# Alternating the score products, moving the weight decoding, and a shorter first pass in an mLSTM + two-layer MLP kernel

## The chip, the cores and the metric

One core of one Trainium2 chip. The metric is the device time of one launch in microseconds: the kernel before takes 467.19 us (median of three runs, 466.68 to 467.29).

## The reference

The inputs are q, k, v and o_gate of shape (2, 8, 768, 40) and i_gate, f_gate of shape (2, 8, 768). An mLSTM runs over the 768 steps of each of the 16 heads:

```
m_new = max(f + m, i);  f_stab = exp(f + m - m_new);  i_stab = exp(i - m_new)
C = f_stab * C + i_stab * outer(v, k)
n = f_stab * n + i_stab * k
y = sigmoid(o) * (C q) / max(|n q|, 1)
```

Its output, 1536 tokens of width 320, goes through two dense layers, each with weights 320 x 2048 in and 2048 x 320 out:

```
h = x @ w_in;  g = h - tanh(h);            x = g @ w_out      # layer 1
h = x @ w_in;  g = h * tanh(softplus(h));  x = g @ w_out      # layer 2
```

## The kernel before

**Attention.** The recurrence is done in chunks of 128 steps: 6 chunks of 2 batch entries make 12 token tiles, each with 8 heads. `attention(j)` (L279) does one of them. It makes the decay matrix in two halves (`nb`, L303 to L319, exponential on ScalarE, L322; mask on GpSimd, L324), the scores of the 8 heads into two PSUM tiles `sc` of 4 heads each (L339), multiplies them by the decay on VectorE (L343), adds the product with the carried state (`it`, L350) to the product with v (`pv`, L361), normalises and gates (L355 to L376; `gated[j]`, L374, is the last of these), and updates the state (`st`, L382; L389, L390). A q or k of heads 0 to 3 lies on partitions 0 to 63, one of heads 4 to 7 on partitions 64 to 127. So a score product uses one half of TensorE's rows, and the two `sc` tiles belong to the two halves. The inputs are float32, and each such product is two MATMUL instructions in the trace: 16 per token tile for the scores. From the MLP's start on, all PSUM tiles of the attention come from one pool of 3 buffers (`ps_at`).

**MLP.** Token tiles are grouped by two into 6 blocks for layer 1, and by four into 3 for layer 2. A weight part is 128 of the 2048 hidden units, 16 parts per layer. The work unit, called a tile here, is of the same size in both layers: in layer 1 a block of 256 tokens by 2 parts, in layer 2 512 tokens by 1 part, 48 of them per layer. For each, `mm1` (L506) makes the hidden values with 16 (layer 1) or 8 (layer 2) MATMULs of L516, `tile1` or `tile2` applies the activation on ScalarE and VectorE and splits the result in a high and a low part, and `mm2` (L561) multiplies by the out weights with 12 MATMULs (L577 to L579), two tiles later.

**Two passes.** Layer 1 goes over the blocks twice. `CUT` (L84) says how many parts a block takes in the first pass, and `segs` (L496) lists the stretches: first pass of blocks 0 to 5, then second pass of blocks 0 to 5 with the other parts. With 8 and 10 parts the first pass has 4 + 5 * 5 = 29 tiles and the second 19. In the first pass over block k the attention of block k+1 is emitted in between, 14 steps per stretch (`ahead`, L752, L794 and L823), since that block's transposed input `xT` (L264 to L267) must be there when the next stretch begins. The attention of block 0 comes before the first tile.

**Decoding.** A weight part arrives as float64 bits (704 KB) and is turned into a high and a low float32 part by `conv_w` (L180): four or five VectorE instructions (L190, L191, L194, L199, L200) with two ScalarE ones between (L192, L197). `conv_to` (L776) emits decodings: up to `CUT[0]` in the first stretch, then evenly over the first pass, `CY` tiles ahead; `mark` is VectorE's first instruction of the latest activation, and the decoding stands behind it in VectorE's queue. In the second pass it emits the first four parts of layer 2. After each decoding the next load is issued on SyncE's queue, into one of 3 buffers (`rawp`).

**Order.** The program is traced in the order of the code, and a planner with its own estimate of times then sets the order of each engine's queue: an instruction that comes later may go first if it is ready earlier. `issue_after` (in `after`, L135) ties an instruction behind another one on its engine; `in_turn` (L142) makes a chain of such ties. On the chip each engine runs its queue in that order.

Of the kernel before, what the change touches and what calls it, by code (L numbers as in the profile page):

```python
# [25 lines left out]
def kernel(  # L26
# [11 lines left out]
    nc = tc.nc  # L38
    B, P, _, HG, S = qk.shape
# [5 lines left out]
    NF, _, WC = w1.shape  # L45
    D1 = D + 1
    HP = P // 2
# [33 lines left out]
    NB = len(blocks1)  # L81


    CUT = [8] + [10] * (NB - 1)  # L84
    M1 = max(BLOCKS) * L
    M2 = max(len(x) for x in flat) * L
    MX = max(NP * M1, M2)
# [39 lines left out]
    last, chain, fill, mark, second = [], [], [], [], []  # L127
# [3 lines left out]
    scored, gated = {}, {}  # L131
# [3 lines left out]
    def after(x):  # L135
        e = ExitStack()
        for i in x:
            e.enter_context(tc.issue_after(i.ins))
        return e

    @contextmanager
    def in_turn(bound=True):  # L142
        done = []

        def turn(issue):
            with after(done[-1:] if bound else []):
                done.append(issue())

        yield turn

    def copy_r(eng, o, x):
        if eng == 0:
            nc.scalar.activation(out=o, in_=x, func=AF.Copy)  # L153
        elif eng == 1:
            nc.vector.tensor_copy(o, x)
        else:
            nc.gpsimd.tensor_scalar(o, in0=x, scalar1=1.0, scalar2=0.0, op0=ALU.mult, op1=ALU.add)
# [6 lines left out]
    def load_w(n=1):  # L164
        for _ in range(n):
            if pending_loads:
                layer, f = pending_loads.pop(0)
                early = layer == 0 and f < ER
                t = (xp if early else rawp).tile(
                    [P, 2 * WC], U32, tag="x" if early else "raw", name="raw", bufs=NB - 1 if early else None  # L170
                )
                with after(spq):
                    x = nc.sync.dma_start(out=t, in_=(w1, w2)[layer][f].bitcast(U32))
                if layer == 0 and f < ER + 3:
                    spq[:] = [x]
                raw[layer, f] = t
# [3 lines left out]
    def conv_w(layer, f, first=(), behind=()):  # L180
        r = raw.pop((layer, f)).rearrange("p (n t) -> p n t", t=2)
        lo32, z = r[:, :, 0], r[:, :, 1]
        zf = z.bitcast(F32)
        w = wp.tile([P, WT], F32R, tag="w", name="w")
        wf = w.bitcast(F32)

        with after(first):
            nc.vector.tensor_scalar(lo32, in0=lo32, scalar1=29, scalar2=None, op0=ALU.logical_shift_right)  # L190
        nc.vector.scalar_tensor_tensor(lo32, in0=z, scalar=0x80000000, in1=lo32, op0=ALU.bitwise_and, op1=ALU.bitwise_or)  # L191
        scaled[layer, f] = nc.scalar.activation(out=zf, in_=zf, func=AF.Copy, scale=2.0 ** -111)  # L192
        with after(behind):
            third[layer, f] = nc.vector.scalar_tensor_tensor(  # L194
                z, in0=z, scalar=3, in1=lo32, op0=ALU.logical_shift_left, op1=ALU.bitwise_or
            )
        cvd[:] = [nc.scalar.activation(out=w[:, 0:WC], in_=zf, func=AF.Copy)]  # L197
        eng = nc.gpsimd if layer == 0 and f < PRE else nc.vector
        eng.tensor_tensor(w[:, WC:WT], in0=zf[:, 0:REM0], in1=wf[:, 0:REM0], op=ALU.subtract)  # L199
        eng.tensor_tensor(w[64:P, REM0:REM1], in0=zf[64:P, REM0:REM1], in1=wf[64:P, REM0:REM1], op=ALU.subtract)  # L200
        wtile[layer, f] = w
# [27 lines left out]
    def load_o(c0, c1):  # L229
        x = xo[:, :, 0:DM].rearrange("p (c b) d -> p c b d", b=B)  # L230
        if c1 - c0 == 1:
            nc.sync.dma_start(out=x[:, c0, :, :], in_=og[:, c0 * L:c1 * L, :].rearrange("b s d -> s b d"))
            return
        for b in range(B):
            nc.sync.dma_start(
                out=x[:, c0:c1, b, :], in_=og[b, c0 * L:c1 * L, :].rearrange("(c s) d -> s c d", s=L)
            )
# [7 lines left out]
    def at_ps(shape, name):  # L245
        p, tag = at_pools[0]
        if len(at_pools) > 1:
            at_pools.append(at_pools.pop(0))
        return p.tile(shape, F32, tag=tag, name=name)
# [29 lines left out]
    def attention(j):  # L279
# [3 lines left out]
        hp = lambda t, h, d=D: t[HP * (h // HG):HP * (h // HG) + d, h % HG, :]  # L283
# [14 lines left out]
        for hf in range(2):  # L298
            nb = at_ps([P, HG, L], "nb")
            flat = nb.rearrange("p g s -> p (g s)")  # L300
            if c < EC:
                bh = b * H + HG * hf
                nc.tensor.matmul(  # L303
                    flat, lhsT=na[c], rhs=sel[:, bh:bh + HG].rearrange("p (g o) -> p g o", o=1).to_broadcast([P, HG, L]),
                    start=True, stop=False,
                )
                for hh in range(HG):
                    nc.tensor.matmul(
                        nb[:, hh, :], lhsT=sel[:, bh + hh:bh + hh + 1].to_broadcast([P, P]), rhs=n0[c], start=False,
                        stop=False,  # L310
                    )

                x = nc.tensor.matmul(
                    nb, lhsT=identr, rhs=cm.rearrange("p (o s) -> p o s", o=1).to_broadcast([P, HG, L]), start=False,
                    stop=True,
                )
# [13 lines left out]
        if c + 1 < NCH:  # L330
            wv = ap_.tile([P, H, D1], F32, tag="wv", name="wv", bufs=2)
# [1 line left out]
            copy_r(2, dl, Dm[:, :, L - 1:L])  # L333
            dls[:] = [nc.gpsimd.tensor_tensor(wv, in0=v, in1=dl.to_broadcast([P, H, D1]), op=ALU.mult)]
        scs = [at_ps([P, HG, L], "sc") for _ in range(2)]
        for hh in range(HG):
            for r, sc in enumerate(scs):
                h = HG * r + hh
                x = nc.tensor.matmul(sc[:, hh, :], lhsT=hp(kT, h, HP), rhs=hp(q, h, HP), start=True, stop=True)  # L339
        yield  # L340
        for r, sc in enumerate(scs):
            d4 = Dm[:, HG * r:HG * r + HG, :]
# [4 lines left out]
        if c > 0:  # L347
            it = at_ps([P, HG, 2, D1], "it")
            for g in range(HG):
                nc.tensor.matmul(  # L350
                    it[:, g].rearrange("p h d -> p (h d)"), lhsT=q[:, g, :],
                    rhs=C[:, g].rearrange("p h d -> p (h d)"), start=True, stop=True,
# [7 lines left out]
        for h in range(H):  # L360
            x = nc.tensor.matmul(pv[:, h, :], lhsT=Dm[:, h, :], rhs=v[:, h, :], start=True, stop=True)  # L361
# [3 lines left out]
        else:  # L365
# [6 lines left out]
        x = xo[:, j, 0:DM].rearrange("p (h d) -> p h d", h=H)  # L372
        nc.vector.tensor_tensor(x, in0=hv[:, :, 0:D], in1=x, op=ALU.mult)
        gated[j] = nc.vector.scalar_tensor_tensor(  # L374
            x, in0=x, scalar=1 / WS, in1=den.to_broadcast([P, H, D]), op0=ALU.mult, op1=ALU.mult
# [2 lines left out]
        yield  # L378
        if c + 1 < NCH:
            st = at_ps([P, HG, D1], "st")  # L380
            for h in [HG * r + g for g in range(HG) for r in range(2)]:
                nc.tensor.matmul(hp(st, h), lhsT=k[:, h, :], rhs=wv[:, h, :], start=True, stop=True)  # L382
            for r in range(2):
                sl = slice(HP * r, HP * r + D)
                if c == 0:
                    copy_r(0, C[sl, :, r, :], st[sl])
                else:
                    dc = dec[sl, b, :, c:c + 1].to_broadcast([D, HG, D1])
                    nc.gpsimd.tensor_tensor(C[sl, :, r, :], in0=C[sl, :, r, :], in1=dc, op=ALU.mult)  # L389
                    nc.vector.tensor_tensor(C[sl, :, r, :], in0=C[sl, :, r, :], in1=st[sl], op=ALU.add)  # L390
# [104 lines left out]

    segs = [(bi, 0, CUT[bi]) for bi in range(NB)] + [(bi, CUT[bi], NF) for bi in range(NB)]  # L496
    tiles = [(0, bi, f) for bi, f0, f1 in segs for f in range(f0, f1, NP)]
# [4 lines left out]
    def span(i):  # L502
        l, bi, f = tiles[i]
        return l, bi, range(f, f + (1 if l else NP)), len(blk[l, bi]) * L
# [27 lines left out]
    def tile1(i):  # L532
# [4 lines left out]

        with after(tbl + ([scaled[0, fs[-1] + 1]] if i < CUT[0] // NP - 1 else [])):
            texp.append(nc.scalar.activation(out=u, in_=h, func=AF.Tanh, scale=G_B))  # L539
# [21 lines left out]
    def mm2(i):  # L561
        l, bi, fs, nt = span(i)
        ends_ = (0,) if l else (0, CUT[bi], NF)
        if fs[0] in ends_:
# [15 lines left out]
        if fs[-1] + 1 in ends_ or fs[-1] == NF - 1:  # L580
            more = l == 0 and fs[-1] + 1 > CUT[bi]
            for t, a in enumerate(accs.pop((l, bi))):
# [27 lines left out]
    def program():  # L610
# [56 lines left out]
        new_xT(0, 0)  # L667

        ga, gb = (attention(j) for j in blk[0, 0])

        def go(g, n=1):
# [22 lines left out]
        start = chain[:]  # L694
        conv1 = [0]

        def lead1(n, x=()):
            while conv1[0] < min(n, NF):
                f = conv1[0]
                with after(x):  # L700
                    conv_w(
                        0, f, [third[0, f - 1]] if f and f < PRE else (), [gated[f]] if f < PRE else ()
                    )
                if conv1[0] >= PRE:
                    load_w()
                if conv1[0] == PRE + 1:
                    with after(spq):
                        load_o(*oc.pop(0))
                conv1[0] += 1
# [56 lines left out]
        seg_at, k = {}, 0  # L766
        for n, (_, f0, f1) in enumerate(segs):
            seg_at[k] = n
            k += len(range(f0, f1, NP))
        n_0 = sum(CUT) // NP  # L770
        n_s = CUT[0] // NP


        CY, R2, E2 = 6, 4, 4

        def conv_to(i, bi, f):  # L776
            if i < n_s:
                lead1(min(CUT[0], f + PRE + NP), start)
            elif i < n_0:
                lead1(CUT[0] + -(-(NF - CUT[0]) * min(i - n_s + CY, n_0 - n_s) // (n_0 - n_s)), mark)  # L780
            elif conv1[0] == NF:
                lead2(min((i - n_0 + 2) // R2, E2))

# [4 lines left out]
        for i in range(len(tiles)):  # L788
# [3 lines left out]
            if l == 0 and i in seg_at:  # L792
                k = seg_at[i]
# [105 lines left out]
```

## Time and profile before

| | us |
|---|---|
| median of three runs | 467.19 |
| the profiled execution | 467.56 |
| its span, first to last instruction | 465.5 |
| PE busy | 449.7 (97%) |
| DVE busy | 321.2 (69%) |
| ACT busy | 285.7 (61%) |
| POOL busy | 115.0 (25%) |

PE is TensorE, DVE VectorE, ACT ScalarE, POOL GpSimd, SP SyncE. The share of busy time is a mean over stages that differ, so it is read by stretches. 2.1 us of the profiled execution lie outside the span.

### The profile page before, as it was taken

The numbers are of one execution on the slowest core, as the hardware profiler recorded it, in microseconds if no ns is written. First come the engines' busy times: TensorE is split into PE (matmuls) and PEld (weight loads), VectorE is DVE, ScalarE is ACT, GpSimd is POOL, SyncE is SP. The second block draws the span as 40 slices with busy tenths as digits, with TensorE's granted clock in tenths as the row PEclk, the third lists the DMA queues.
The fourth block names the chain that finished last, engine by engine and source line by source line (L and its number), as shares of the span: only waits on it lengthen the run. The fifth ranks groups of instructions, "written<-read, shape, count | busy, mean of one in ns | idle before, by whom it ended". The sixth has DMA issues, their size and how long they took to land.

```text
span 465.5 us, 8005 instructions
## 1 busy us (share of the span) xinstructions
PE 449.7 (97%) x3103; PEld 407.8 (88%) x3103; DVE 321.2 (69%) x546; ACT 285.7 (61%) x518; POOL 115.0 (25%) x121
## 2 busy tenths in 40 slices
PE   9968979999999999999999999999999999999997
PEld 5645869999989999999999989988889988998896
DVE  7997999989888887666889977989943221221112
ACT  6878556596665865888889787666643322332232
POOL 3313535475354431342433332000000000000000
PEclk9999999999999999999999999999999999999999
DMA  7964453513506111000120110435301000010001
GB/s 249 353 246 155 144 164 128 179 37 108 165 4 182 29 63 63 1 1 1 63 64 0 63 63 1 131 127 182 121 1 56 2 0 1 0 58 0 1 0 56
DMA packets 22744, 38.03 MB, mean 82 GB/s; under 512 B 1364, under 2 KB 17044, under 8 KB 22708
## 3 DMA queue, kind: packets, MB, share of 16 engines
q1 hardware_dynamic: 22708, 37.54, 24.5%
q8 instruction: 24, 0.39, 0.3%
q14 instruction: 12, 0.10, 0.1%
HBM read 35.41 MB, written 1.97 MB: 80 GB/s over the span
## 4 chain that ended last, share of the span: by engine, by line
PE 64%; DVE 18%; issue 7%; ACT 4%; POOL 3%; DMA 2%; POOLq 0%; SPq 0%; ACTq 0%; DVEq 0%
PE h L516 28%; PE acc L577 9%; PE acc L578 9%; PE acc L579 9%; DVE raw L194 3%; PE sc L339 3%; POOL gl L529 3%; DMA raw<-in_w_dram 2%; PE pv L361 2%; DVE raw L191 2%; DVE w L199 2%; DVE raw L190 2%; DVE w L200 2%; DVE gl L558 1%; PE xt L264 1%
## 5 line engine op out<-in xcount | busy, mean ns | idle before, releaser
L516 PE MATMUL h<-xT,w 128*128 128x256 f32 (+1 forms) x1152 | 210.9, 323 | 7.5 <-ACT w L197 4.2
L516 PEld LDWEIGHTS h<-xT,w 128*128 128x128 f32 x1152 | 169.0, 189 | 25.5 <-ACT w L197 6.2
L577 PE MATMUL acc<-w,gh 128*128 128x320 f32 x384 | 118.6, 312 | 0.8 <-DVE xo L594 0.8
L578 PE MATMUL acc<-w,gh 128*128 128x320 f32 x384 | 118.2, 310 | 0.0
L579 PE MATMUL acc<-w,gl 128*128 128x320 f32 x384 | 109.9, 310 | 0.0
L529 POOL TENSOR_TENSOR gl<-g,gh 128x512 fp32r<-128x512 f32 x48 | 66.0, 1377 | 120.8 <-ACT gh L153 115.1
L558 DVE TENSOR_TENSOR gl<-g,gh 128x512 fp32r<-128x512 f32 x48 | 33.1, 691 | 86.8 <-ACT g L557 86.7
L577 PEld LDWEIGHTS acc<-w,gh 128*128 128x128 f32 x384 | 72.0, 188 | 3.5 <-ACT w L197 1.0
L556 ACT ACTIVATE gh<-h 128x512 fp32r<-128x512 f32 x48 | 28.8, 599 | 75.4 <-PE h L516 74.9
L578 PEld LDWEIGHTS acc<-w,gh 128*128 128x128 f32 x384 | 72.2, 188 | 2.3
L579 PEld LDWEIGHTS acc<-w,gl 128*128 128x128 f32 x384 | 69.7, 188 | 1.5 <-issue 0.4
L545 DVE COPY_PREDICATED g<-u,t 128x512 f32<-128x512 uint32 x48 | 40.5, 846 | 10.0 <-ACT u L544 9.9
L542 DVE TENSOR_TENSOR g<-u,h 128x512 f32<-128x512 f32 x48 | 32.7, 681 | 16.9 <-ACT u L541 13.4
L153 ACT ACTIVATE gh<-g 128x512 fp32r<-128x512 f32 x48 | 30.5, 635 | 19.7 <-DVE g L545 15.4
L544 ACT ACTIVATE u<-u,bias 128x512 f32<-128x512 f32 x48 | 34.9, 727 | 11.4 <-DVE g L542 11.4
L197 ACT ACTIVATE w<-raw 128x704 fp32r<-128x704 f32 x32 | 27.5, 861 | 16.2 <-DVE raw L194 16.0
L539 ACT ACTIVATE u<-h 128x512 f32<-128x512 f32 x48 | 28.5, 593 | 11.7 <-PE h L516 11.6
L192 ACT ACTIVATE raw<-raw 128x704 f32<-128x704 f32 x32 | 27.6, 864 | 11.1 <-DVE raw L191 10.0
L543 DVE TENSOR_TENSOR t<-h,t 128x512 f32<-128x512 f32 x48 | 32.8, 683 | 0.0
L194 DVE SCALAR_TENSOR_TENSOR raw<-raw 128x704 uint32<-128x704 uint32 x32 | 30.9, 964 | 2.6 <-ACT raw L192 2.4
L541 ACT ACTIVATE u<-u 128x512 f32<-128x512 f32 x48 | 30.6, 638 | 0.0
L199 DVE TENSOR_TENSOR w<-raw,w 128x576 fp32r<-128x576 f32 x30 | 27.5, 915 | 2.9 <-ACT w L197 2.4
(103 smaller groups left out, 496.8 us busy)
## 6 DMA issues: line engine op xcount, KB each, us to landing
raw<-in_w_dram SPq DMA_DIRECT2D x32, 704.0 KB
qk_t<-in_qk_dram SPq DMA_DIRECT2D x12, 512.0 KB
kv_t<-in_kv_dram SPq DMA_DIRECT2D x12, 324.0 KB
out_dram<-xo SPq DMA_DIRECT2D x12, 160.0 KB
xo<-in_og_dram SPq DMA_DIRECT2D x2, 640.0 KB
xo<-in_og_dram SPq DMA_DIRECT2D x2, 320.0 KB
sd<-nr SPq DMA_DIRECT2D x20, 4.0 KB
md<-nr SPq DMA_DIRECT2D x10, 8.0 KB
```

Source lines behind the costliest of these rows:

```text
L194: third[layer, f] = nc.vector.scalar_tensor_tensor(z, in0=z, scalar=3, in1=lo32, op0=ALU.logical_shift_left, op1=ALU.bitwise_or)
L199: eng.tensor_tensor(w[:, WC:WT], in0=zf[:, 0:REM0], in1=wf[:, 0:REM0], op=ALU.subtract)
L516: y = nc.tensor.matmul(t[:, k * nt:(k + 1) * nt], lhsT=w[:, o:o + P], rhs=x[:, kk, :], start=(n == 0), stop=(n == len(pairs) - 1),)
L529: nc.gpsimd.tensor_tensor(gl, in0=g, in1=gh.bitcast(F32), op=ALU.subtract)
L542: mark[:] = [nc.vector.tensor_tensor(g, in0=u, in1=h, op=ALU.mult)]
L543: nc.vector.tensor_tensor(t, in0=h, in1=t, op=ALU.subtract)
L544: nc.scalar.activation(out=u, in_=u, func=AF.Relu, bias=bias[:, 0:1])
L545: nc.vector.copy_predicated(out=g, mask=u.bitcast(U32), data=t)
L558: mark.append(nc.vector.tensor_tensor(gl, in0=g, in1=gh.bitcast(F32), op=ALU.subtract))
L577: turn(lambda: nc.tensor.matmul(a, lhsT=gh[:, sl], rhs=wh, start=(f in ends_), stop=False))
L578: turn(lambda: nc.tensor.matmul(a, lhsT=gh[:, sl], rhs=wl, start=False, stop=False))
L579: turn(lambda: nc.tensor.matmul(a, lhsT=gl[:, sl], rhs=wh, start=False, stop=end))
```

## The change

The scores' products are chained in the order head 4, 0, 5, 1, ..., so that each stands behind the one before it on TensorE's queue. The state update's products (already traced in alternation) are chained too. The first pass takes 6 parts of block 0 and 8 of the others: 3 + 5 * 4 = 23 tiles, and the second 25. `CY` is 4, not 6. From the second stretch on, a decoding also stands behind the newest `gated` that has been emitted by then.

```diff
-    CUT = [8] + [10] * (NB - 1)
+    CUT = [6] + [8] * (NB - 1)
@@ attention
-        for hh in range(HG):
-            for r, sc in enumerate(scs):
-                h = HG * r + hh
-                x = nc.tensor.matmul(sc[:, hh, :], lhsT=hp(kT, h, HP), rhs=hp(q, h, HP), start=True, stop=True)
+        with in_turn() as turn:
+            for hh in range(HG):
+                for r in (1, 0):
+                    h = HG * r + hh
+                    turn(lambda: nc.tensor.matmul(scs[r][:, hh, :], lhsT=hp(kT, h, HP), rhs=hp(q, h, HP), start=True, stop=True))
...
-            for h in [HG * r + g for g in range(HG) for r in range(2)]:
-                nc.tensor.matmul(hp(st, h), lhsT=k[:, h, :], rhs=wv[:, h, :], start=True, stop=True)
+            with in_turn() as turn:
+                for h in [HG * r + g for g in range(HG) for r in range(2)]:
+                    turn(lambda: nc.tensor.matmul(hp(st, h), lhsT=k[:, h, :], rhs=wv[:, h, :], start=True, stop=True))
@@ program
-        CY, R2, E2 = 6, 4, 4
+        CY, R2, E2 = 4, 4, 4
...
-                lead1(CUT[0] + -(-(NF - CUT[0]) * min(i - n_s + CY, n_0 - n_s) // (n_0 - n_s)), mark)
+                lead1(
+                    CUT[0] + -(-(NF - CUT[0]) * min(i - n_s + CY, n_0 - n_s) // (n_0 - n_s)), mark + [gated[max(gated)]]
+                )
```

## Rows read from the trace of the kernel before

**Rows 1.** The page's busy time of each engine: us, share, instructions.
```profile
PE 449.7 (97%) x3103; PEld 407.8 (88%) x3103; DVE 321.2 (69%) x546; ACT 285.7 (61%) x518; POOL 115.0 (25%) x121
```
**Rows 2.** Busy time by stretches: start:end, length, then each engine, clock, DMA.
```profile
23.60:66.80 43.20, 35.10 (x253) 27.02 (x253) 40.43 (x70) 29.58 (x49) 14.88 (x18) 0.96 0.56 187
66.80:188.00 121.20, 120.45 (x990) 113.81 (x991) 105.99 (x189) 81.14 (x158) 56.88 (x58) 1.00 0.30 92
188.00:276.20 88.20, 87.36 (x674) 87.18 (x673) 72.35 (x111) 73.69 (x137) 29.56 (x23) 1.00 0.10 34
72.00:84.00 12.00, 12.00 (x97) 11.50 (x97) 11.91 (x19) 8.05 (x16) 6.19 (x7) 1.00 0.53 168
```
**Rows 3.** The same stretches, instructions on tile h alone: PE, PEld, DVE, ACT.
```profile
23.60:66.80 43.20, 12.52 (x65) 9.59 (x65) 5.12 (x8) 4.32 (x8) 0.96 0.56 187
66.80:188.00 121.20, 46.29 (x320) 41.19 (x321) 24.05 (x38) 20.60 (x38) 1.00 0.30 92
188.00:276.20 88.20, 51.96 (x386) 49.08 (x385) 29.77 (x47) 25.14 (x47) 1.00 0.10 34
```
**Rows 4.** The chain of waits, 41 to 67 us: start, us, what.
```profile
41.97 0.53 DVE raw L190
...
50.95 1.25 DVE w L199
52.22 0.29 DVE w L200
...
57.54 1.27 DVE w L200
...
60.73 0.50 DVE xo L374
...
61.37 0.41 PE xt L264 x2
...
66.79 0.98 PE h L516 x6
```
**Rows 5.** The chain of waits, attention's products on PE.
```profile
8.68 1.14 PE sc L339 x16
...
102.83 1.42 PE sc L339 x16
...
128.73 0.24 PE nb L319
...
129.68 1.08 PE sc L339 x8
...
141.61 0.85 PE it L350 x8
142.46 1.75 PE pv L361 x16
...
147.47 0.44 PE st L382 x16
```
**Rows 6.** The chain of waits, one activation on DVE.
```profile
77.57 0.68 DVE g L542
78.25 0.60 DVE t L543
...
81.48 0.75 DVE g L545
```
**Rows 7.** 66.8 to 188, instructions on tile raw alone: DVE, ACT, POOL.
```profile
66.80:188.00 121.20, 32.07 (x38) 13.70 (x16) 0.00 (x0) 1.00 0.30 92
```
**Rows 8.** DVE's groups by line, 66.8 to 188: count, busy, mean ns, idle before.
```profile
L199 DVE TENSOR_TENSOR w<-raw,w 128x576 fp32r<-128x576 f32 x8 | 8.4, 1052 | 1.5 <-ACT w L197 1.5
L267 DVE TENSOR_TENSOR xT<-xt,xT 128x384 fp32r<-128x384 f32 x9 | 5.0, 552 | 2.1 <-ACT xT L266 2.0
L200 DVE TENSOR_TENSOR w<-raw,w 64x128 fp32r<-64x128 f32 x8 | 4.3, 532 | 0.1
```
**Rows 9.** The same groups, 300 to 340, where POOL is idle.
```profile
L199 DVE TENSOR_TENSOR w<-raw,w 128x576 fp32r<-128x576 f32 x9 | 6.8, 756 | 1.5 <-ACT w L197 0.9
...
L200 DVE TENSOR_TENSOR w<-raw,w 64x128 fp32r<-64x128 f32 x9 | 2.6, 289 | 0.3
```
**Rows 10.** POOL's costliest group, 66.8 to 188.
```profile
L529 POOL TENSOR_TENSOR gl<-g,gh 128x512 fp32r<-128x512 f32 x19 | 27.3, 1441 | 40.0 <-ACT gh L153 39.8
```
**Rows 11.** The chain of waits, a late weight load in layer 2.
```profile
324.85 4.68 DMA raw<-in_w_dram
```
**Rows 12.** The chain of waits, transposes of blocks 2 and 3.
```profile
93.61 0.41 PE xt L264 x2
94.02 1.53 PE h L516 x13
```

## The prediction

> **What bounds the kernel now.** I read the page's busy times first, then the busy time by stretches, then the chain of waits and the groups by line inside the stretches that the change touches. The page says PE 97% and DVE 69% [rows 1]; the stretches say where that holds. From 23.6 to 66.8 us, the first four tiles, PE is busy for 35.1 of 43.2 us, while DVE is busy for 40.43 [rows 2]: DVE bounds it, and the reader sees in the chain that it runs through decodings (L190 to L200) up to the gating (L374 at 60.73), on to the transposes and to the first tile of the second stretch at 66.79 [rows 4]. From 66.8 to 188 PE has no idle time worth the name (120.45 of 121.2), DVE 106.0 [rows 2]. MATMULs on h count the tiles, 16 each: 320 here, so 20 tiles, four blocks of five; 386 from 188 to 276.2, so 24 tiles [rows 3]. In that last stretch nothing but tiles stands on PE: 88.2 / 24 = 3.675 us a tile. Block period from 66.8 to 188: 121.2 / 4 = 30.3 us. Layer 2 begins at about 276.2, and what follows isn't touched: its decodings, loads and tiles are the same in number and order.
>
> **The PE work of a block.** Five tiles are 5 * 3.675 = 18.4 us. One token tile's attention on PE, in pieces of the chain [rows 5, 12]: scores 2 * 1.08 (two runs of 8), `it` 0.85, `pv` 1.75, `st` 0.44, `nb` 2 * 0.24, transposes 0.41; together 6.1, two of them 12.2. Sum 30.6 against the 30.3 measured: PE's own work explains the period, no wait is needed.
>
> **Scores in alternation.** The trace holds both orders: 16 products take 1.14 us at 8.68, where the two halves alternate, and 8 in one run take 1.08 at 129.68; 102.83 is a mixture, 1.42 [rows 5]. The change makes every token tile 1.14 where two runs took 2.16: 1.02 less on PE. The three token tiles before 47 us alternate already. In the four blocks of 66.8 to 188 that is close to 8 us, in the place where PE is the bound. It has a price: the first product now waits until both score buffers are free, and the first of the two multiplications on DVE, which could start after the first run, starts after the pair. The second score tile ends no later than before, so I take 0; the other end, that this sets the block's period, is a rival.
>
> **State products chained.** They run in 0.44 us for 16 [rows 5], alternating already. 0.
>
> **Fewer parts in the first pass.** The number of tiles, evictions and decodings stays. What moves:
>
> - The first stretch has 3 tiles and 6 decodings to wait for. The decodings of parts 6 and 7 leave it. Eight of their pieces stand on the chain between 41.97 and 60.7, the first 0.53, the two longest 1.25 and 1.27 [rows 4], 6.1 us in all; the fourth tile's products and activation between the two transposes go as well. Late next is the attention of block 1 itself. Bounds for the start of the second stretch: 66.8, if the attention's latency sets it, and 56.8, if all that DVE drops (two decodings of 4.2 and a tile of 1.95, below) is gained. I take 59.5, nearest to the chain's own pieces with a little for the tile.
> - A block of stretches 2 to 5 has four tiles: PE 4 * 3.675 + 2 * 5.1 = 24.9 us.
> - After the last attention there are 48 - 19 = 29 tiles, not 24, at 3.675: 106.6 us.
>
> **What this asks of DVE.** An activation is 0.60 + 0.60 + 0.75 = 1.95 us [rows 6] (L542 runs 0.08 into its successor). Decoding in 66.8 to 188: 32.07 us for 38 instructions, 7.6 decodings, 4.2 each [rows 7]. The rest is attention: (105.99 - 19 * 1.95 - 32.07) / 8 = 4.6 a token tile, transposes included [rows 2, 7]. A block before: 106 / 4 = 26.5, hidden under PE's 30.3. A block after: 4 * 1.95 + 9.2 + 2 decodings (10 over 20 tiles) 8.4 = 25.4, against PE's 24.9. The cover is gone: two engines with nearly the same load. DVE has been 94% busy over the first stretch and 99% at best (11.91 of 12) [rows 2]; at 98% the block takes 26.0. The first of the four has parts 6 and 7 to decode at once, and 8 before its second gating, half a decoding more than two: 27.5. Four blocks: 27.5 + 3 * 26.0 = 105.5. ACT, at 81 of 121 us before, stays under it.
>
> **Decoding behind the gating, CY.** Parts 8 to 15 are wanted only in the second pass, so a decoding that stands behind the newest gating delays no product; it lets the gating go first. In front of what waits stand on DVE only the attention's own instructions, and behind it the activations, whose hidden values have 3 buffers. Cost 0; the bounds are a decoding more or less per block on the attention's path, 4.2 us, and are inside the range. Each decoding also issues the next weight load on SP, ahead of some q, k, v loads and gate copies. Sixteen loads stay sixteen, over a shorter time, DMA share 0.30 [rows 2]; one late load costs up to 4.7 us [rows 11]. I take 0, as the rows of the first pass show none.
>
> A rule bears on the price of a decoding. Beside GpSimd the two steps with two SBUF inputs are longer: L199 1.052 and L200 0.532 us from 66.8 to 188, with POOL busy for 47% of it, against 0.756 and 0.289 from 300 to 340 without POOL [rows 2, 8, 9], 0.54 us per decoding. POOL's share after is (56.88 / 4 - 1.44) / 26.0 = 49% (one L529 less a block [rows 10]), so 4.2 us per decoding stands. The Trainium skill (SBUF — State Buffer, Who interferes with whom) says that a DVE instruction with two SBUF inputs and a GpSimd instruction that reads SBUF exclude each other, the later one waiting for the whole of the other; the trace agrees. By that rule the place of a decoding sets its price, and the change moves it: if each of the ten met one whole L529, it would cost 1.44 - 0.54 = 0.9 us more, and the forecast would be 9 us higher, 471.6; clear of POOL it would be 0.54 less, which ends at the first rival below.
>
> **Sum.** 59.5 + 105.5 + 106.6 = 271.6 against 276.2: 4.6 us less. The profiled execution of 467.56 (span 465.5 and 2.1 outside) becomes 463.0; it is 0.4 over the median, so the median of 467.19 becomes 462.6.
>
> **Rivals.**
>
> - *DVE gives way.* Decodings slip behind, into the second pass, where DVE has 15.9 of 88.2 us free [rows 2], and the block runs at PE's 24.9: 59.5 + 99.6 + 106.6 = 265.7, median 456.7. For it: PE showed no wait in 121 us beside a DVE at 87%. Against: the stretch where DVE is over 94% has PE idle.
> - *The attention's latency sets the block, slower.* A block's attention goes from its first `nb` to its transposes (128.73 [rows 5] to about 155) through 3 PSUM buffers, two token tiles in turn; now a score pair also holds one buffer while it waits for the other. If the period stays at 30.3 though only 24.9 of PE work is left in it, PE idles for 5 us in each of four blocks, and the tiles that left the first pass come afterwards in full: 59.5 + 121.2 + 106.6 = 287.3, median 478.3. It decides from a period of 27.5 up: 59.5 + 110.0 + 106.6 = 276.1, and nothing is left of the gain. For it: transposes at 93.61 run straight into the next stretch's tiles [rows 12], so the slack is small. Against: PE's work alone explains 30.3, so the trace shows no latency that long.
> - *The first stretch doesn't shorten.* Second stretch at 66.8 with all else as forecast: 278.9, median 469.9, slower. For it: block 1's products wait on a chain of masks, scores and normalisations; against: the chain there is DVE's work and mostly decodings.
> - *The chain does little.* If the planner puts other products between the pairs and scores stay at 2.16, PE has 26.9 a block and the period is about 27.0 (28.5 for the first): 59.5 + 109.5 + 106.6 = 275.6, median 466.6, no change.
>
> **Chances.** Changes within 0.2% (0.93 us) can't be told from none here. Forecast 0.52 (its own range 458 to 466.5, nearly all of it faster), DVE gives way 0.20, latency 0.14, first stretch 0.08, chain does little 0.06. Faster by over 0.2%: 0.50 + 0.20 = 0.70; same 0.02 + 0.06 + 0.03 (the mild end of the third rival) = 0.11; slower 0.14 + 0.05 = 0.19. The range 455 to 471 leaves out most of the latency rival and the far end of the second: about 0.17.
>
> **What would show it.** After: L339's 16 products in runs of about 1.1 us in every token tile; 48 MATMULs on h before the second stretch's first tile, at 57 to 62 us; its four blocks of 64 MATMULs at 25 to 28 us each, DVE over 95% busy in them; 29 tiles at 3.67 then; layer 2 at about 271. If PE has gaps in the blocks that end at ACT's or DVE's attention steps while DVE is under 90%, the latency rival holds; if DVE is full and PE waits, the cover was worth more than I gave it. I am wrong altogether if layer 2's stretch changes its length.

## The result and the profile after

The change makes the kernel slower: 472.96 us (median of four runs, 470.84 to 474.45) against 467.24 before, ratio 1.0114 with a 95% interval of 1.0086 to 1.0142. The forecast was 462.6, range 455 to 471, and faster.

The profiled execution took 470.84 us, span 468.9; before, 467.56 and 465.5. It is the fastest of the four, with the highest mean granted TensorE clock: 0.993 with 470.84, 0.986 with 472.94, 0.985 with 472.98, 0.981 with 474.45. So the other three executions took 2.1 to 3.6 us more and carry a lower mean clock, that is, more time at the lower of its two levels (1.2 GHz instead of 2.4); there is no trace of them.

The page's busy times after (us, share of the span, instructions):

```profile
PE 447.3 (95%) x3103; PEld 402.3 (86%) x3103; DVE 317.6 (68%) x546; ACT 285.3 (61%) x518; POOL 106.1 (23%) x121
```

Line numbers are those of the changed kernel, which stand up to four further down: L340 is L339 of before, L375 is L374, L518 is L516. Against [rows 1] PE is busy for 2.4 us less, 95% of the span instead of 97%. Busy time by stretches after (start:end, length, PE, PEld, DVE, ACT, POOL, clock, DMA share, GB/s): first stretch, the four blocks with attention, the rest of layer 1, layer 2.

```profile
24.30:63.10 38.80, 33.26 (x234) 24.78 (x234) 30.37 (x57) 24.65 (x43) 12.09 (x17) 0.91 0.50 163
63.10:175.40 112.30, 104.99 (x892) 95.87 (x892) 99.41 (x184) 74.69 (x142) 46.69 (x55) 1.00 0.33 101
...
175.40:281.40 106.00, 104.17 (x800) 103.80 (x801) 85.93 (x135) 87.66 (x162) 36.10 (x28) 1.00 0.13 42
281.40:468.90 187.50, 182.85 (x1022) 164.21 (x1020) 81.66 (x131) 80.81 (x142) 3.26 (x3) 1.00 0.13 46
```

The same with the instructions on tile h alone, whose PE count tells the tiles, 16 each:

```profile
63.10:175.40 112.30, 35.69 (x256) 32.07 (x256) 20.54 (x32) 17.61 (x32) 1.00 0.33 101
175.40:281.40 106.00, 61.98 (x464) 59.02 (x465) 35.77 (x56) 30.17 (x56) 1.00 0.13 42
```

256 are 16 tiles, four blocks of four: 112.3 / 4 = 28.1 us a block, where [rows 2] had 30.3 for blocks of five. 464 are the 29 tiles that follow, 3.66 us each. Layer 2 begins at 281.4, not 276.2: 3.7 us won up to the second stretch (63.1, not 66.8), 8.9 lost from there on. PE has 7.3 us without an instruction in the four blocks, where before it had 0.75 in four longer ones, and DVE isn't full either: 99.4 of 112.3 us, 88.5%. PE's busy time itself is 26.2 us a block, over the 24.9 put forward: MATMULs overlap (at 115 us those of `mm2` start 0.15 us apart and last 0.31), so a short wait of PE need not show as a gap.

The scores do alternate. A row of the chain of waits after (start, us, what), the answer to [rows 5]:

```profile
98.84 1.09 PE sc L340 x16
```

And DVE's decoding in the four blocks, instructions on tile raw alone: 43 instructions, 8.6 decodings, 3.9 us each, the answer to [rows 7].

```profile
63.10:175.40 112.30, 33.28 (x43) 16.39 (x19) 0.00 (x0) 1.00 0.33 101
```

Whom PE waited for in these blocks (engine, line, waited for: us in all, times, longest):

```profile
PE h L518 <- ACT xT L266: 2.2, 3, 1.0
PE nb L319 <- ACT Dm L322: 1.7, 3, 0.7
PE nb L319 <- DVE xT L267: 1.7, 3, 1.0
PE h L518 <- ACT u L546: 0.7, 1, 0.7
PE sc L340 <- DVE xT L267: 0.6, 1, 0.6
```

The same view of the kernel before, from 66.8 to 188, has three such rows of PE, together 1.2 us. After, 6.2 of the 6.9 us stand at the seam of two blocks: the next block's tile waits for the transposed input, and its decay matrix (`nb`) and scores wait for a PSUM buffer, which the exponential or the transposes' second half (L267, on DVE) sets free. What stands in front of L267 is seen in DVE's timeline at such a seam (start, us, engine, line, operation, tiles, shapes, count):

```profile
115.26 0.48 DVE L375 SCALAR_TENSOR_TENSOR xo<-xo,den 128x320 f32<-128x320 f32 x1
115.67 0.52 DVE L190 TENSOR_SCALAR raw<-raw 128x704 uint32<-128x704 uint32 x1
...
116.22 0.89 DVE L191 SCALAR_TENSOR_TENSOR raw<-raw 128x704 uint32<-128x704 uint32 x1
...
117.26 0.49 DVE L375 SCALAR_TENSOR_TENSOR xo<-xo,den 128x320 f32<-128x320 f32 x1
117.67 0.52 DVE L190 TENSOR_SCALAR raw<-raw 128x704 uint32<-128x704 uint32 x1
118.10 0.88 DVE L194 SCALAR_TENSOR_TENSOR raw<-raw 128x704 uint32<-128x704 uint32 x1
...
119.72 0.89 DVE L191 SCALAR_TENSOR_TENSOR raw<-raw 128x704 uint32<-128x704 uint32 x1
120.65 0.56 DVE L267 TENSOR_TENSOR xT<-xt,xT 128x384 fp32r<-128x384 f32 x1
121.12 0.75 DVE L199 TENSOR_TENSOR w<-raw,w 128x576 fp32r<-128x576 f32 x1
121.88 0.63 DVE L200 TENSOR_TENSOR w<-raw,w 64x128 fp32r<-64x128 f32 x1
122.54 0.56 DVE L267 TENSOR_TENSOR xT<-xt,xT 128x384 fp32r<-128x384 f32 x1
```

The gatings (L375) begin at 115.26 and 117.26. Steps of two decodings follow and come between, and the two L267 begin at 120.65 and 122.54, 2.1 and 1.4 us after ACT's half of the same transposes (L266, which they read) ended at 118.53 and 121.10. In DVE's groups of the last three blocks it has no wait of its own any more (idle before: 0.1 us, against 2.1 in [rows 8]); its input is there, and it stands in the queue behind the decodings:

```profile
L267 DVE TENSOR_TENSOR xT<-xt,xT 128x384 fp32r<-128x384 f32 x7 | 3.8, 552 | 0.1
```

The four blocks differ among themselves. Instructions on tile raw alone, block by block:

```profile
63.10:92.90 29.80, 9.91 (x13) 4.47 (x6) 0.00 (x0) 1.00 0.39 116
92.90:121.60 28.70, 8.85 (x12) 4.43 (x6) 0.00 (x0) 1.00 0.37 112
121.60:147.20 25.60, 5.93 (x9) 3.29 (x4) 0.00 (x0) 1.00 0.42 125
147.20:175.40 28.20, 8.59 (x11) 4.20 (x5) 0.00 (x0) 1.00 0.16 53
```

The block with the least decoding, 5.9 us, is the shortest, 25.6 us; the others have 8.6 to 9.9 us and take 28.2 to 29.8. It also has 12 products of `mm2` fewer than each of the others, worth some 1.6 us at 3.675 us for the 28 of a tile, so this row alone doesn't prove the cause.

### The profile page after: what moved, and what is told of

Read it like the earlier page. It is cut to its first block, busy times and chain, and to the rows that moved or that the text cites. A ratio compares the mean times of both kernels' runs of the same rounds, so it can differ in the third digit from the quotient of the medians.

```text
span 468.9 us, 8027 instructions
## 1 busy us (share of the span) xinstructions
PE 447.3 (95%) x3103; PEld 402.3 (86%) x3103; DVE 317.6 (68%) x546; ACT 285.3 (61%) x518; POOL 106.1 (23%) x121
## 4 chain that ended last, share of the span: by engine, by line
PE 39%; issue 22%; DVE 19%; POOL 10%; ACT 6%; DMA 3%; POOLq 0%; SPq 0%; ACTq 0%; DVEq 0%
PE h L518 17%; POOL gl L531 9%; PE acc L581 5%; PE acc L579 5%; PE acc L580 5%; DMA raw<-in_w_dram 3%; DVE raw L191 2%; DVE raw L194 2%; PE sc L340 2%; DVE raw L190 2%; PE w_ps L619 2%; DVE w L199 2%; ACT raw L192 1%; DVE w L200 1%; PE pv L362 1%
## 5 line engine op out<-in xcount | busy, mean ns | idle before, releaser
L518 PE MATMUL h<-xT,w 128*128 128x256 f32 (+1 forms) x1152 | 208.0, 323 | 12.3 <-ACT w L197 4.1
L518 PEld LDWEIGHTS h<-xT,w 128*128 128x128 f32 x1152 | 167.8, 189 | 31.0 <-ACT w L197 6.1
L581 PE MATMUL acc<-w,gl 128*128 128x320 f32 x384 | 107.9, 312 | 0.0
L560 DVE TENSOR_TENSOR gl<-g,gh 128x512 fp32r<-128x512 f32 x48 | 33.2, 691 | 87.7 <-ACT g L559 87.6
L531 POOL TENSOR_TENSOR gl<-g,gh 128x512 fp32r<-128x512 f32 x48 | 63.3, 1321 | 125.5 <-ACT gh L153 125.3
L558 ACT ACTIVATE gh<-h 128x512 fp32r<-128x512 f32 x48 | 28.8, 600 | 79.8 <-PE h L518 79.4
L547 DVE COPY_PREDICATED g<-u,t 128x512 f32<-128x512 uint32 x48 | 38.6, 812 | 8.0 <-ACT u L546 7.8
L153 ACT ACTIVATE gh<-g 128x512 fp32r<-128x512 f32 x48 | 30.4, 632 | 20.4 <-DVE g L547 19.3
L197 ACT ACTIVATE w<-raw 128x704 fp32r<-128x704 f32 x32 | 27.3, 860 | 12.4 <-DVE raw L194 12.1
L543 ACT ACTIVATE u<-u 128x512 f32<-128x512 f32 x48 | 30.5, 638 | 0.0
L199 DVE TENSOR_TENSOR w<-raw,w 128x576 fp32r<-128x576 f32 x30 | 27.0, 898 | 4.4 <-ACT w L197 3.6
```

Source lines behind the costliest of these rows:

```text
L518: y = nc.tensor.matmul(t[:, k * nt:(k + 1) * nt], lhsT=w[:, o:o + P], rhs=x[:, kk, :], start=(n == 0), stop=(n == len(pairs) - 1),)
L531: nc.gpsimd.tensor_tensor(gl, in0=g, in1=gh.bitcast(F32), op=ALU.subtract)
L547: nc.vector.copy_predicated(out=g, mask=u.bitcast(U32), data=t)
L560: mark.append(nc.vector.tensor_tensor(gl, in0=g, in1=gh.bitcast(F32), op=ALU.subtract))
L581: turn(lambda: nc.tensor.matmul(a, lhsT=gl[:, sl], rhs=wh, start=False, stop=end))
```

## The experiments

Each kernel's ratio is to the kernel before, run beside it on the same chip. "Block" is the mean period of the four blocks with attention, read from its profile as above; there is one profile of each kernel. Single blocks of one kernel differ by up to 4 us (25.6 to 29.8 above), so where blocks 2 to 4 alone are compared, the text says so and the table at the end has both.

**The three parts one by one.** Theories: S, a block of four tiles is shorter than its attention; G, the decoding queued behind the gating delays the next block; C, the chain costs by itself.

Chains alone, `e1`: the two `in_turn` hunks of the diff.

> The kernel before with the two chains alone (scores and state products in turn); CUT 8/10, CY 6, decoding behind mark only. Theory S (short first pass: a block of four tiles leaves less TensorE work than the attention takes to come through): the chain takes about 8 us off TensorE's work in four blocks, but blocks of five tiles then also come down towards the attention's latency of about 28 us; 461 to 466. Theory G (decoding behind the gating stands ahead of the transposes on VectorE and delays the next block): 459 to 463, the chain's gain in full. Theory C (the chain itself costs, since a pair waits for both score buffers): 468 or more.

471.36 us, 1.0075 (1.0050 to 1.0101): the time that theory C names, but not by its reason. The chain of five-tile blocks does gain: 28.65 us a block against 30.3. But its second stretch begins at 73.9, not 66.8. DVE's timeline there shows why: activations and two decodings of the next stretch stand between the second token tile's `hv` sums (60.7) and its gating at 70.56. No wait of a score product is on record for PE between 45 and 75 us; the longest is one of 3.5 us for an activation (L153).

```profile
62.53 0.95 DVE L190 TENSOR_SCALAR raw<-raw 128x704 uint32<-128x704 uint32 x2
...
67.27 1.51 DVE L191 SCALAR_TENSOR_TENSOR raw<-raw 128x704 uint32<-128x704 uint32 x1
...
69.75 0.89 DVE L194 SCALAR_TENSOR_TENSOR raw<-raw 128x704 uint32<-128x704 uint32 x1
70.56 0.49 DVE L375 SCALAR_TENSOR_TENSOR xo<-xo,den 128x320 f32<-128x320 f32 x1
```

Shorter first pass alone, `e2`:

```diff
-    CUT = [8] + [10] * (NB - 1)
+    CUT = [6] + [8] * (NB - 1)
-        CY, R2, E2 = 6, 4, 4
+        CY, R2, E2 = 4, 4, 4
```

> The kernel before with the shorter first pass alone (CUT 6/8, CY 4). Theory S: slower, 471 to 478, blocks of about 28 us or more with waits on TensorE. Theory G: not the culprit, 464 to 468. Theory C: 464 to 468.

472.91 us, 1.0107 (1.0079 to 1.0134): as slow as the whole change. Second stretch at 66.5, blocks of 27.8 us. So the shorter first pass alone doesn't bring the second stretch forward. Instructions on tile raw in the first stretch (DVE, ACT, POOL) of the kernel before, of `e2` and of the changed kernel:

```profile
23.60:66.80 43.20, 24.46 (x32) 9.88 (x12) 1.76 (x2) 0.96 0.56 187
23.50:66.50 43.00, 21.24 (x30) 9.78 (x12) 1.78 (x2) 0.87 0.57 189
24.30:63.10 38.80, 15.38 (x22) 6.43 (x8) 1.75 (x2) 0.91 0.50 163
```

In `e2` decodings of the next stretch take the place of those that left: 30 instructions, where the kernel before has 32 and the changed one 22. It is the decoding behind the gating that keeps them out; `e15` below has it without the chains and 23 such instructions, 16.0 us, and its second stretch begins at 63.1. Some of the 3.4 us between `e2` and `e15` can be the clock, 0.87 here and 0.91 there: by an estimate from these two means, up to 2 us.

Decoding behind the gating alone, `e3` (`mark + [gated[max(gated)]]`):

> The kernel before with the decoding queued behind the newest gating alone. Theory G: slower, 469 to 473, the VectorE half of the transposes (L267) later behind its gating (L374) than the 0.5 to 4.6 us of the kernel before. Theory S and theory C: 466 to 468.

466.65 us, 0.9985 (0.9970 to 1.0000): no difference that is clear of the interval, with blocks of 30.2 us. G fails for blocks of five.

The change without it, `e4`:

> The changed kernel without the queueing of the decoding behind the gating (chains, CUT 6/8, CY 4 stay). Theory G: 460 to 465, at least 8 us under the changed kernel's 473. Theory S: 470 to 474, as the changed kernel. Theory C: 470 to 474.

486.31 us, 1.0401 (1.0374 to 1.0429), outside all three ranges and 13 us over the changed kernel: G is wrong, and the opposite holds. Second stretch at 67.6, blocks of 30.9 us. PE waits in them for ACT's and POOL's halves of the activation's result, whose DVE steps now come late, and its granted clock is 0.93 over the stretch, 1.2 GHz in part:

```profile
67.60:191.20 123.60, 111.88 (x903) 102.60 (x901) 95.58 (x180) 76.74 (x144) 45.20 (x56) 0.93 0.31 94
```

```profile
PE acc L579 <- ACT gh L153: 6.6, 4, 1.9
PE acc L581 <- POOL gl L531: 2.1, 3, 0.7
PE xt L264 <- DVE den L372: 1.6, 1, 1.6
```

A mean of 0.93 over 123.6 us is some 17 us at the lower level, in which PE does half the work: an estimate of up to 8.7 of the 11.3 us by which these four blocks are longer than the changed kernel's. Waits and clock aren't taken apart by any run.

**Pairs.** Chains and gating with the first pass of before, `e5`:

> The changed kernel with the first pass of before (CUT 8/10, CY 6): chains and decoding behind the gating alone. Theory L (a block of four tiles is shorter than what its attention takes, about 28 us; one of five is not): blocks of five tiles at TensorE's own 28.6 us, the second stretch at 67, layer 2 at about 270, 459 to 463. Theory X (the chain costs by itself, as the 471 of the chain alone suggests): 468 to 472.

468.80 us, 1.0029 (1.0010 to 1.0048), in theory X's range, but the blocks, 29.15, are near L's 28.6; it is the first stretch that is again long (27.0 to 73.7, with a spell at the lower clock in it). Only block 0's pass shorter, `e6` (`CUT = [6] + [10] * (NB - 1)`, CY 6):

> As the changed kernel, but only block 0 has the shorter first pass (CUT 6/10, CY 6): a first stretch of three tiles, blocks of five. Theory L: second stretch at 63, four blocks of 28.6, then 25 tiles of 3.675, layer 2 at 269.3: 457 to 462. If the first pass is bad because its first stretch is short: 468 or more.

472.87 us, 1.0112 (1.0082 to 1.0143). It begins its second stretch at 62.8 as forecast, and the next block takes 36.4 us, where the kernel before took 31.0. Three decodings end in it at 72.0 to 75.3, and PE waits 1.7 us for an activation behind them. In this kernel, what the short first stretch wins is given back one block later.

Shorter pass and gating without the chains, `e15`:

> The shorter first pass (CUT 6/8, CY 4) with decoding behind the gating, no chain: the changed kernel without its chains. Theory D (in a block of four tiles the decodings and the attention on VectorE set 28 us, so the chain's saving on TensorE is idle time): 470 to 474, as with the chains, blocks of about 28. If the chain's gain does come out there: 476 or more. If the chain costs: 466 to 469.

468.30 us, 1.0014 (0.9994 to 1.0034), blocks of 27.4. It falls in none but the last of the expectations: in blocks of four tiles the chains don't just gain nothing, the kernel with them is 4.7 us slower. The two profiles show 2.8 us of that, in the four blocks (112.3 against 109.5), and all of it in the first: 29.8 against 26.1, while blocks 2 to 4 take 27.5 with the chains and 27.8 without. e15's first block holds 28 products of `mm2`, the changed kernel's 48, which is 2.6 us of the 3.7 at a tile's 3.675 us for 28; over all four blocks it is 168 against 180, 1.6 us of the 2.8. So little of a price of the chains is seen in the blocks, and the rest of the 4.7 us stays open.

**What fills a block of four.** Behind the transposes, `e7`:

```diff
-mark + [gated[max(gated)]]
+mark + [gated[max(gated)]] + chain[2:]
```

> The changed kernel, the decoding also behind the newest VectorE half of a transpose (L267). Theory G (decodings between the gating and the transposes make a block longer): blocks of 25 to 26.5 us instead of 28.1, 463 to 467. Theory L: blocks of 27.5 or more, 470 to 474.

476.63 us, 1.0209 (1.0171 to 1.0247), blocks of 28.5 (2 to 4: 27.5, as in the changed kernel). So it isn't the one place of the decodings at the seam: moved from it, they cost as much elsewhere.

Decodings out of the blocks, `e9`, run twice. The first run gave 486.38 us, and its profiled execution, at 1102.65 us, can't be read; the second is read here:

```diff
-            elif i < n_0:
+            elif i < n_0 - 4:
+                lead1(8, mark + [gated[max(gated)]])
+            elif i < n_0 + 4:
+                lead1(9 + i - (n_0 - 4), mark + [gated[max(gated)]])
+            elif i < 0:
```

> The kernel of e9_late_decoding again, for its profile: the decoding of parts 8 to 15 is taken out of the four blocks. Theory D (VectorE's decodings fill the block): second to fourth blocks at 25 us. Theory L: 27.5 or more. The time, 486 before, is not the point.

486.15 us, 1.0393 (1.0346 to 1.0440), a little over the 470 to 485 that were expected of the first run for what comes later. The second to fourth blocks, whole and with the MATMULs on h alone:

```profile
91.80:168.60 76.80, 76.22 (x658) 71.39 (x656) 52.03 (x106) 46.33 (x94) 29.44 (x39) 1.00 0.17 50
```

```profile
91.80:168.60 76.80, 28.91 (x192) 24.98 (x191) 15.43 (x24) 13.04 (x24) 1.00 0.17 50
```

192 MATMULs, three blocks in 76.8 us: 25.6 each, against 27.5 for the same three of the changed kernel. Both have the same products on PE there: 192 on h, 132 of `mm2`, 96 of the scores. No wait of PE is on record in them; PE is busy for 76.2 of 76.8 us and is the bound. D holds: without the decodings the alternation's gain comes out, since 25.6 is under the 26.8 of the work without it.

A fourth PSUM buffer for the attention, `e8` (`PS = [2, 2, 4]`):

> The changed kernel with 4 PSUM buffers for the attention and 2 for the hidden values, not 3 and 3. Theory B (the attention waits for its three PSUM buffers): blocks of 25 to 26.5 us instead of 28.1. Theory L (its own steps and their places in the queues): 27.5 or more. The hidden values have a buffer less, which can cost time in the 29 tiles after the attention, so the blocks are to be read, not the sum.

470.18 us, 1.0047 (1.0028 to 1.0067). Second to fourth blocks, and the changed kernel's:

```profile
95.30:172.00 76.70, 74.82 (x648) 70.21 (x647) 73.92 (x130) 50.24 (x100) 31.17 (x36) 0.99 0.33 103
```

```profile
92.90:175.40 82.50, 77.17 (x657) 71.07 (x657) 72.53 (x135) 55.42 (x105) 33.85 (x39) 1.00 0.31 96
```

25.6 us a block here too, with the decodings in place (25.2 us on tile raw, against 23.4), and DVE at 73.9 of 76.7, 96%, where three buffers leave it at 72.5 of 82.5, 88%. Whom PE waits for in these blocks:

```profile
PE nb L319 <- ACT Dm L322: 0.9, 2, 0.6
PE h L518 <- ACT xT L266: 0.6, 1, 0.6
PE h L518 <- DVE t L545: 0.3, 2, 0.2
```

The waits for a buffer that L267 sets free, 1.7 and 0.6 us in the changed kernel, are gone. So B holds for these three blocks. Over all four it doesn't come out by the number: 27.6 us, since the first takes 33.6 at a mean clock of 0.88 (some 8 us at the lower level, an estimate of up to 4 us). These three blocks hold 81 score products, not 96 (the rest, about 1 us, falls into the first one), and 140 of `mm2`, not 132. The two findings are one, as far as blocks 2 to 4 go: DVE's steps set the buffers free, decodings stand in front of those steps, and with three buffers PE and then DVE itself wait for the next one. Less in DVE's queue or one more buffer breaks the circle. In `e8` the queues are also ordered anew, with a buffer less for the hidden values; that is not taken apart. The 29 tiles behind the blocks take 108.4 us there, not 106.0, so the sum gains less.

The attention emitted earlier, `e10` (`0.8` for `0.4` in the lead of L827, L823 of before):

> The changed kernel with the attention's steps emitted 0.8 of a stretch ahead, not 0.4. If a block's period is a latency that starts when its steps are emitted: blocks of 25 to 26 us, 463 to 466. If the attention's own chain has no room for an earlier start (one block's transposes are followed at once by the next block's first products): 27.5 or more, 470 to 475.

468.84 us, 1.0026 (1.0004 to 1.0049), between the expectations, and blocks of 28.1. But the first of them, 32.0 us, runs at a mean clock of 0.89; blocks 2 to 4, at 1.00, take 26.8, where the changed kernel takes 27.5. So emission doesn't set the whole period, and a part of it isn't ruled out. Its profiled execution is its slowest (471.22, clock 0.974), so where its median gains 4 us on the changed kernel stays open.

**Longer blocks instead.** Six tiles, chains and gating, `e11`:

```diff
-    CUT = [6] + [8] * (NB - 1)
+    CUT = [8] + [12] * (NB - 1)
-        CY, R2, E2 = 4, 4, 4
+        CY, R2, E2 = 8, 4, 4
```

> Chains and decoding behind the gating, with a longer first pass instead (CUT 8/12, CY 8): blocks of six tiles. Theory L: TensorE's work of a block, 6 * 3.675 + 2 * 5.0 = 32.1 us, is above the attention's 28, so no wait is left in the four blocks and the chain's gain comes out: second stretch at 67 to 73, four blocks of 32.1, then 20 tiles of 3.675, layer 2 at 269 to 275, 458 to 465. If the chain costs by itself whatever the block: 468 to 473.

465.77 us, 0.9961 (0.9945 to 0.9977): faster than both kernels, and 0.8 us above the range. Blocks, 384 MATMULs on h are four of six tiles:

```profile
71.70:200.60 128.90, 126.91 (x1089) 120.07 (x1088) 111.15 (x196) 90.14 (x175) 54.28 (x61) 1.00 0.28 87
```

```profile
71.70:200.60 128.90, 53.29 (x384) 48.61 (x384) 29.24 (x46) 25.02 (x46) 1.00 0.28 87
```

32.2 us a block, against 32.1 put forward from PE's work. The same without chains, `e13`:

> Six tiles a block with decoding behind the gating, no chain at all. If the 465.8 of the six-tile kernel is the chain's gain in blocks that TensorE bounds: here blocks of 6 * 3.675 + 12.1 = 34.1 us, 466 to 468. If a longer first pass by itself is better: 463 to 465.

471.43 us, 1.0088 (1.0056 to 1.0120), blocks of 34.2:

```profile
66.60:203.40 136.80, 134.81 (x1102) 126.88 (x1103) 118.04 (x202) 93.15 (x178) 60.21 (x62) 1.00 0.27 82
```

The blocks are as expected (34.1), and layer 2 begins at 276.0, as before; the 4 us of the time come behind that, in a layer 2 of 193.2 us (before 189.3). The chains' gain on blocks is 2.0 us each; up to 0.4 of that is `mm2`, of which 252 products fall into e11's blocks and 264 into e13's. And e11's blocks begin 5.1 us later (71.7 against 66.6), so of the 7.9 us that they win, 2.1 are left where layer 2 begins (273.9 against 276.0).

Chains only from the third block's attention on, `e12` (`in_turn(j >= 4)`, the old order below):

> Six tiles a block with decoding behind the gating, the chains only from the third block's attention on, so that the first stretch keeps the order of before. Theory F (the chain lengthens the first stretch, 71.7 against 66.8, and gains in the four blocks): second stretch at 67, four blocks of 32.2, 20 tiles of 3.675: layer 2 at 269, 459 to 463. If the first stretch is long for another reason (CY 8, three decodings at once): 465 to 467 as with the chain throughout.

465.64 us, 0.9961 (0.9939 to 0.9983). Second stretch at 67.3 as forecast, but blocks of 33.1: what the start wins the blocks give back. Theory F is half right; the time is the one of the other expectation. With CY 7, `e14`:

> As e12_six_chain_later with CY 7: two decodings, not three, are emitted as the second stretch begins. Theory F: as e12 within 1 us. If the crowd of decodings at the start of the second stretch is what lengthens it: 2 to 4 us less than e12.

475.27 us, 1.0175 (1.0136 to 1.0215), 10 us more for one tile less of lead, with blocks of 33.2 and layer 2 at 274.9, near e12's 273.0. The loss is in layer 2, which the edit doesn't touch: 198.6 us, against 190.7 in e12. Its queues run in another order: PE's products wait there for the activation on ACT (L558), 3.8 us in five waits, which e12's trace doesn't have.

The first decodings of layer 2 earlier, R2 = 3, in e11 (`e16`) and e12 (`e17`):

> The six-tile kernel with the chains throughout and the first decodings of layer 2 every 3 tiles (R2 = 3), not 4, so that four of them, not three, stand ready when layer 2 begins. If the 189.6 us of its layer 2 hide a late fourth decoding: 463 to 465. If layer 2's length is set by the other twelve: 465 to 467, no change.

> The same with the chains from the third block's attention on (e12 with R2 = 3), whose layer 2 took 190.7 us: 462 to 464 if the fourth decoding was late there, 465 to 467 if not.

471.48 us, 1.0081 (1.0061 to 1.0101), and 470.80, 1.0081 (1.0058 to 1.0104): slower, layer 2 in 193.8 and 193.4 us, 4.2 and 2.7 more than in e11 and e12, and it begins some 2 us later. Neither expectation holds, and no gain of a late decoding shows. What in the order costs the time wasn't looked into.

The blocks side by side (PE's work is 3.675 a tile and 12.1 for two attentions, or 10.2 with the scores in alternation):

| kernel | tiles | scores chained | decoding behind gating | PE's work | four blocks | blocks 2 to 4 |
|---|---|---|---|---|---|---|
| before | 5 | no | no | 30.5 | 30.3 | 30.1 |
| e13 | 6 | no | yes | 34.2 | 34.2 | 34.0 |
| e11 | 6 | yes | yes | 32.2 | 32.2 | 32.2 |
| e1 | 5 | yes | no | 28.6 | 28.65 | 29.1 |
| e5 | 5 | yes | yes | 28.6 | 29.15 | 29.4 |
| e2 | 4 | no | no | 26.8 | 27.8 | 27.7 |
| e15 | 4 | no | yes | 26.8 | 27.4 | 27.8 |
| after | 4 | yes | yes | 24.9 | 28.1 | 27.5 |
| e4 | 4 | yes | no | 24.9 | 30.9 | 30.7 |
| e7 | 4 | yes | yes, and behind L267 | 24.9 | 28.5 | 27.5 |
| e10, emitted earlier | 4 | yes | yes | 24.9 | 28.1 | 26.8 |
| e8, a fourth buffer | 4 | yes | yes | 24.9 | 27.6 | 25.6 |
| e9 | 4 | yes | late | 24.9 | 26.4 | 25.6 |

"PE's work" counts every tile with all its products. In the traces some of `mm2`'s come after the blocks (216 of 240 fall into them before, 180 of 192 after, 252 of 288 in e11, 264 of 288 in e13), so at 3.675 us for 28 products it is 0.4 to 1.2 us a block too high. The exact agreement of the two columns in the upper rows is partly chance.

## Why the prediction was wrong

- **The step that failed is DVE's share of a block**: "at 98% the block takes 26.0", four blocks in 105.5 us. They took 112.3. The loads were sized rightly: 99.41 / 4 = 24.9 us of DVE work against 25.4 put forward, decodings of 3.9 us against 4.2. What was wrong is that two engines with nearly the same load, tied together by three PSUM buffers and one in-order queue, could both be kept full over whole blocks. DVE reached 88.5%. I had taken 98% from 94% over the first stretch, where PE was idle for 8.1 of 43.2 us, and from 99% over 12 us, in which PE was full too [rows 2]; 12 us don't speak for a block with its seam. Shown, for blocks 2 to 4, by e8 (96%, 25.6 us) and e9 (25.6). The 27.5 for the first block also left out the 98%: 25.4 and half a decoding are 28.1 with it; it took 29.8.
- The rival that names the latency of a block through 3 PSUM buffers, with 27.5 us as the point from which it decides, is what happened, at 28.1 rather than its 30.3, and its sign came too: gaps of PE at ACT's and DVE's attention steps with DVE under 90%. I gave it 0.14, arguing that PE's work alone explains the 30.3 of before. That is about true (its sum counts 24 products of `mm2` too many, 0.8 us a block) and no evidence: a block bound by PE hides any shorter latency.
- **Scores in alternation**: right as an operation, 1.09 us for 16. Right as a gain where PE is the bound (2.0 us a block of six, e11 against e13, with some of it `mm2`, as said), nearly so in blocks of five (28.65 in e1 and 29.15 in e5, from 30.3), none in blocks of four (28.1 with, 27.4 without, e15). With 8 parts in the first stretch the chains lengthen that stretch, by 5.1 us in e11 against e13, which I hadn't looked for. The price that I put at 0, a pair waiting for both buffers, is not shown: PE's waits have 0.6 us of it in the four blocks, and the 4.7 us between e15 and the changed kernel hold all effects of the chains on the order, 1.6 of them `mm2`'s products that come later in e15.
- **First stretch**: 63.1, not 59.5. The cause was wrong too: I let the two decodings leave because of the shorter pass, and with that alone (e2) the stretch still holds 30 of 32 decoding instructions and ends at 66.5, with up to 2 us of clock in it, by the estimate above. They leave by standing behind the gating, which I put at 0 (after: 22 instructions); then about half of what they held on the chain comes out. e15 begins at 63.1 as well, so the chains have no part in it. In e6 the gain is given back in the next block; in e15, whose first block takes 26.1 us, it isn't.
- **Decoding behind the gating at 0**: wrong. It is worth 13 us where the blocks are short and chained (e4 against the changed kernel), through the start (67.6 against 63.1) and through blocks of 30.9 us, with the clock at 0.93 in them; 4.6 us where they are short and not chained (e2 against e15); nothing in the kernel before (e3).
- **29 tiles at 3.675**: right, 106.0 against 106.6. Layer 2, put at no change, took 187.5, not 189.3, so the sign "I am wrong altogether if layer 2's stretch changes its length" came, by 1.8 us in the kernel's favour. Its code is the same; what in its order gains them wasn't looked into.
- The sum in the prediction's terms, for the profiled execution: 463.0 + 3.6 (start) + 6.8 (blocks) - 0.6 - 1.8 = 471.0, measured 470.84. The median's 2.1 us above that execution, where before's stood 0.3 under its own, goes with a lower mean clock.
- The rule on DVE and GpSimd (the Trainium skill, SBUF — State Buffer, Who interferes with whom) gave no higher price here: a decoding went from 4.2 to 3.9 us, inside the 0.54 less that I had named for one clear of GpSimd. POOL was busy for 42% of these blocks, not 49%, and L199 took 0.900 us in blocks 2 to 4, not 1.052.

## What to carry to other kernels

Work taken from the bounding engine gains only as far as the next bound, so before shortening a stage, look for what its period would be with that engine free, and give it that much cover: here the alternation paid up to 2 us a block with six tiles around it and nothing with four. Don't forecast two engines that share a few buffers at 98% each from a short row: here they reached 93% and 88% over four blocks with three buffers, and 98% and 96% over three with four. And where a planner orders the queues, an edit in one stage moves others: layer 2 varied from 187.3 (e4) to 198.6 us (e14) among kernels that don't differ in it, so a few us of difference need a profile before they get a cause.

## What the runs showed of the hardware

- Float32 products of 64 rows that alternate between the two halves of the array take half the time here: 16 in 1.09 us, 8 in one run 1.08 [rows 5].
- Executions of one kernel differ in the clock: the changed kernel's mean ran from 0.993 to 0.981 over four of them and its time from 470.84 to 474.45 with it, some 0.3 us for each thousandth.
- In e4's blocks, where single waits of PE were up to 1.9 us, the clock was 0.93; in the changed kernel's, where they were up to 1.0 us, it was 1.00.
